# First batch of an FFT filter with a routed expert layer: logits from the spectrum, one index chain, gates in four chunks

## The chip, the cores and the metric

One core of a Trainium2 chip runs the whole program. Its engines are TensorE (PE, with its weight loads as PEld), VectorE (DVE), ScalarE (ACT), GpSimd (POOL) and SyncE (SP, which here only starts transfers). The metric is the device time of one execution in microseconds, as the median of three runs. One further execution was profiled, and its trace gives the rows below.

## What is computed

```
X = rfft(x, axis=1)                      # x: 8 batches x 2496 tokens x 256
y = irfft(X * (filt_r + 1j*filt_i))      # 19968 rows of 256
xn, en = y / |y|, emb / |emb|            # 8 experts
logits = xn @ en.T / tau
e = argmax(logits); gate = softmax(logits)[e]
out = gate * (relu(y @ w1[e]) @ w2[e])   # w1: 256x1024, w2: 1024x256 per expert
```

## The kernel before

**Stages of a batch.** The program handles the eight batches as groups 0 to 7. The transform is a mixed-radix product: `conv_s1` multiplies the input by a table (tiles `s`), `conv_s2` transforms again (`s`, `xs`, `yy`), multiplies by the filter and transforms back (`sa`), and `conv_sb` makes the rows. A group has 11 tiles of two blocks (22 blocks of up to 117 tokens). For each tile `conv_sb` takes a block of the filtered spectrum (`vt`, 120 frequencies by 512), makes `y` by the product with the table `csb` (fp32), sums the squares on ACT into `ssq` (L795), takes a power-of-two scale `rr` from them with two small DVE operations (`q`, `rr`, L798 and L800), and writes the row as a high half (ACT, L766) and a low half in fp16 (DVE, L769). Eight PE transposes turn the tile (`tp`, L828), DVE copies it out (`yT`, L830), and eight small fp16 products with the normalised experts (`ent`, `enz`) give the logits `lp` (L843).

**Routing.** `route` works on a chunk of tiles. The index chain on DVE finds the maximum, a one-hot `oh`, the rank of each row in its expert (products `rk` on PE, L931 to L934), and the row number `ixi`. The gates need the norm of the row: `norm_steps` (L165 to L181) is a chain of small dependent operations, followed by f, d, an exp on ACT, `se` and a reciprocal (L952). Then POOL scatters the rows to `XS` in DRAM, two indirect transfers per tile, 22 per group (L965). In group 0 the constant `FIRST` cuts the 11 tiles into chunks of 3, 4 and 4; the norms of the first two chunks run on POOL (`gates(nc.gpsimd)`), that of the last on DVE.

**Experts.** Each group then has eight expert slots of 256 rows: SP reads the rows back transposed (`xT`, L1101), PE makes `ph` with the first weights (L1134), ACT and DVE make the two halves of `h` (L1140, L1141), PE makes `po` (L1162), and the result goes out by POOL. Each slot has four parts, so that ph_2_1 is the second part of slot 2.

**Weights.** The weights of each expert come as fp32 and are cut into fp16 halves once. `weight_halves` does it in small steps: maxima (`wmx` on DVE L288, `wj` on ACT L285), a product `pm` that transposes them (L295), a product `ps` that spreads them (L305), then the high halves (ACT, L325) and low halves (DVE L330; for one of the four pieces POOL, L323 and L328).

**What sets the order.** In group 0 nothing leaves the chip between the first product and the rows: `conv_first` keeps the spectrum in `turned`, and `turn_back` (L620) transposes it block by block (`v`, copied to `vt` by ACT, L623). `head()` runs 35 steps of `conv_first`, then `conv_sb(0)`, and from a given step on (`S1AT`) also the first stage of group 1, `conv_s1(1)`. For the head the program's order is the engines' order for ACT, PE, DVE and SP. `WLOADS` and `PREPS` list the steps after which a weight load or a preparation step is issued. After the head a planner with costs of its own places the slots, the stages of the next group and what is left of the preparation, one preparation step at each call of `spread`.

Of the kernel before, what the change touches and what calls it, by code (L numbers as in the profile page):

```python
# [43 lines left out]
FIRST = (0, 3, 7, 11)  # L44
# [11 lines left out]
PREPS = (21, 25, 46, 48, 51, 53, 58, 58, 59, 60, 63, 63, 63, 63, 64, 64, 66, 67, 67, 68, 68, 69, 70, 70)  # L56
S1AT = 62
# [3 lines left out]
def moe_spectral_kernel(  # L61
# [125 lines left out]

    def experts_ready():
# [26 lines left out]
        nc.vector.tensor_copy(enz[:, :, 0:E], ept[:, 0:2, 0:E])  # L215
        yield
# [215 lines left out]
    def load(q, g, pool, tag, t, ap, rows, full):  # L432
        if pool is rowp:
            it = pool.tile([P, 2, ROW], F16, tag="rows", name=f"{tag}{g}_{t}").rearrange("p j c -> p (j c)")
            it = it.bitcast(F32)[:, :2 * D].rearrange("p (j c) -> p j c", j=2)
        else:
            it = pool.tile([P, 2, D], F32, tag=tag, name=f"{tag}{g}_{t}")
        got = []
        for h, k, m in whole(g, ap, t, rows, full):
            q.dma_start(it[:k, h], m)  # L440
            got.append((h, it[:k, h].rearrange("p j c -> p (j c)")))
        return got
# [273 lines left out]

    def conv_sb(g):
# [4 lines left out]
        def load_v(t):  # L722
            return load(nc.sync, g, cf, "f", t, buf_at(g, ZD[g]), freqs, 120) if g else turn_back(t)

        ahead = 3 if g else 1
        if g:
            yield W_GAP
        vin = {t: load_v(t) for t in range(ahead)}
        if g:
            yield W_GAP  # L730
        parts, out_rows = [], []
        starts = FIRST if g == 0 else tuple(range(0, NTL, CHUNK)) + (NTL,)
# [8 lines left out]
        def part():  # L741

            if parts and next(parts[0], None) is None:
                parts.pop(0)
            for _ in range(len(out_rows) if g == 0 else min(1, len(out_rows))):
                out_rows.pop(0)()
# [3 lines left out]
        for s in range(NTL + LPL):  # L750
# [22 lines left out]
            if t < NTL:  # L773
                c, at, n = chunk(t)
                if at == 0:
# [12 lines left out]
                y = (ps_o if g == 0 and t % 3 == 2 else ps_y).tile(  # L788
                    [P, 2, D], F32, tag="o" if g == 0 and t % 3 == 2 else "y", name=f"y{g}_{t}")
# [12 lines left out]
                if g == 0 and u + 2 == n:  # L802
                    sg, n0, f = (rt.tile([P, NTC], F32, tag=tag, name=f"{tag}0_{t}")[:, :n] for tag in ("sg", "n0", "f"))

                    def gates(w, sg=sg, n0=n0, f=f, ssq=ssq[:, :n], rr=rr[:, :n]):
                        for _ in norm_steps(sg, ssq, n0, w):
                            pass
                        w.tensor_tensor(out=sg, in0=sg, in1=rr, op=ALU.mult)
                        w.tensor_scalar(out=f, in0=sg, scalar1=tau64, scalar2=None, op0=ALU.mult)
# [10 lines left out]
            if g == 0 and s == NTL + 1:  # L820
                gates(nc.vector)
# [32 lines left out]
    def route(g, out_rows, t0, n, rows, ssq, rr, lp, f=None):  # L854
# [12 lines left out]
        def bc(t):  # L867
            return t.unsqueeze(2).to_broadcast([P, nt, E])
# [5 lines left out]
        if g:  # L874
            sg, n0, f = sm("sg"), sm("n0"), sm("f")
        norm = norm_steps(sg, ssq, n0) if g else iter(())
# [14 lines left out]
        if g:  # L891
            yield 1
# [13 lines left out]
        if g:  # L906
            v.scalar_tensor_tensor(out=f, in0=sg, scalar=tau64, in1=rr, op0=ALU.mult, op1=ALU.mult)
            v.reciprocal(f, f)
            v.tensor_tensor(out=d, in0=d, in1=bc(f), op=ALU.mult)
        ex = big("ex")  # L910

        def gates():
            if g == 0:
                v.reciprocal(f, f)
                v.tensor_tensor(out=d, in0=d, in1=bc(f), op=ALU.mult)
            nc.scalar.activation(ex, d, AF.Exp)

        late = g == 0 and not part_
        if late:
            yield 1  # L920
        else:
            gates()
            if g:
                yield 1
# [18 lines left out]
        if g == 0:  # L943
            v.tensor_copy(ixi, ix)
        if late:
            gates()
            yield 1
# [6 lines left out]
        def rows_out(u, k):  # L954

            if g:
                with behind("conv"):
                    v.tensor_copy(ixi[:, u:u + 1], ix[:, u:u + 1])
            scatter_rows(g, rows[u // 2][:k, u % 2].bitcast(I32), ixi[:k, u:u + 1])
# [239 lines left out]
    def head():  # L1199
        yield from conv_first()  # L1200
        s1 = conv_s1(1)
        next(s1)
        n = 0
        for w in conv_sb(0):
            yield w
            n += 1
            if n > S1AT - 35:
                next(s1, 0)
        yield from s1
# [173 lines left out]
```

## Time and profile before

| | |
|---|---|
| median of three runs (1399.37 to 1404.8) | 1400.31 us |
| the profiled execution | 1404.15 us |
| its span in the trace | 1402.2 us |
| PE busy | 1282.1 us, 91% |
| DVE, ACT, POOL busy | 901.4, 745.9, 548.1 us |

The span runs from the first to the last instruction; the profiled execution's own time is 2 us more. Busy time of PE counts a matmul from its start to a modelled end, so a stretch with 100% need not be at PE's peak. The granted clock is given as a share of the upper level of 2.4 GHz; 0.50 is the lower level, 1.2 GHz.

### The profile page before, as it was taken

How to read it: one execution, taken by the hardware profiler on the slowest of the kernel's cores; microseconds unless marked ns; L12 is line 12 of the kernel's file. 1: busy time of each engine (PE TensorE's matmuls, PEld its weight loads, DVE VectorE, ACT ScalarE, POOL GpSimd, SP SyncE). 2: the span in 40 equal slices, each digit the busy share in tenths (PEclk: the TensorE clock that was granted, in tenths of full speed). 3: DMA queues.
4: the chain of work that ended last, by engine and by line, in shares of the span. 5: the costliest groups of instructions: out<-in, count | busy, mean ns of one | idle time of the engine just before them, and what ended most of it. 6: DMA issues, size and time to landing. Idle time of an engine off the chain costs nothing. (4 is left out here: it accounts for less than half of the span.)

```text
span 1402.2 us, 32774 instructions
## 1 busy us (share of the span) xinstructions
PE 1282.1 (91%) x11308; PEld 1017.4 (73%) x11308; DVE 901.4 (64%) x2850; ACT 745.9 (53%) x1714; POOL 548.1 (39%) x622
## 2 busy tenths in 40 slices
PE   8858999579989997999899989998999899999997
PEld 6535666346767886788687768776787678999997
DVE  3777669554757695758576858685768532366664
ACT  5755377255626773767376737673665223333332
POOL 3363334634353334443543454345423532222221
PEclk9967999889999998999899989998999999999999
DMA  9838855567657664876487557754762322221221
GB/s 326 296 115 245 247 144 154 171 181 212 182 159 188 194 174 138 217 181 193 135 238 182 173 147 209 200 169 133 215 161 64 88 76 46 50 52 48 47 51 35
DMA packets 223256, 218.77 MB, mean 156 GB/s; under 512 B 125022, under 2 KB 168445, under 8 KB 221164
## 3 DMA queue, kind: packets, MB, share of 16 engines
q1 hardware_dynamic: 194491, 156.06, 41.3%
q0 software_dynamic: 25584, 57.79, 13.5%
q10 hardware_dynamic: 3009, 2.75, 0.6%
q8 instruction: 94, 1.54, 0.5%
q14 instruction: 78, 0.64, 0.2%
HBM read 116.43 MB, written 79.60 MB: 140 GB/s over the span
## 5 line engine op out<-in xcount | busy, mean ns | idle before, releaser
L1162 PE MATMUL po<-W,h 128*128 128x256 f16 (+1 forms) x3864 | 522.9, 279 | 22.6 <-issue 21.9
L1162 PEld LDWEIGHTS <-h 128*128 128x128 f16 x3864 | 371.5, 100 | 121.2 <-issue 75.1
L1134 PE MATMUL ph<-xT,W 128*128 128x256 f16 x3072 | 410.5, 279 | 30.0 <-issue 14.9
L1140 ACT ACTIVATE h<-ph 128x512 f16<-128x512 f32 (+1 forms) x388 | 204.1, 528 | 328.7 <-PE ph L1134 156.1
L1134 PEld LDWEIGHTS <-W 128*128 128x128 f16 x3072 | 297.1, 100 | 111.9 <-issue 73.7
L1141 DVE SCALAR_TENSOR_TENSOR h<-ph,h 128x512 f16<-128x512 f32 (+1 forms) x388 | 231.7, 598 | 210.9 <-ACT h L1140 174.5
L1066 POOL DMA_INDIRECT out_dram<-o,meta x161 | 172.7, 1073 | 350.4 <-ACT o L1169 297.7
L965 POOL DMA_INDIRECT XS<-rows,ixi x176 | 179.1, 1018 | 147.3 <-issue 90.9
L693 POOL TENSOR_TENSOR yy<-yy,xs 128x512 f32<-128x512 f32 x48 | 68.4, 1425 | 124.6 <-DVE xs L658 83.1
L440 POOL DMA_DIRECT2D in<-in_x x72 | 56.3, 783 | 131.3 <-PE s L480 47.3
L1134 PE MATMUL ph<-xT,wp 128*128 128x128 f16 x1584 | 104.9, 219 | 0.0
L1134 PEld LDWEIGHTS <-wp 128*128 128x128 f16 x1584 | 96.7, 98 | 2.7 <-issue 0.2
L1169 ACT ACTIVATE o<-po,meta 128x256 f32<-128x256 f32 x161 | 69.9, 477 | 32.9 <-PE po L1162 22.7
L1120 DVE COPY wp<-W 128x1024 f16 x132 | 58.2, 441 | 44.1 <-PE ph L1134 43.2
L766 ACT ACTIVATE rows<-y,rr 128x256 f16<-128x256 f32 x176 | 74.2, 485 | 20.1 <-DVE rr L800 15.9
L769 DVE SCALAR_TENSOR_TENSOR rows<-y,rr,rows 128x256 f16<-128x256 f32 x176 | 76.7, 478 | 12.4 <-ACT rows L766 11.0
L656 DVE TENSOR_TENSOR yy<-s,f 128x256 f32<-128x256 f32 x140 | 53.1, 419 | 39.4 <-ACT xs L686 20.4
L795 ACT ACTIVATE rows<-y 128x256 f16<-128x256 f32 x176 | 66.7, 393 | 19.0 <-PE y L480 11.5
L516 ACT COPY s<-s 128x512 f32<-128x512 f32 x74 | 43.9, 598 | 61.1 <-PE s L480 19.8
L830 DVE COPY yT<-tp 128x1024 f16<-128x1024 f16 x88 | 60.3, 685 | 16.4 <-remote 12.6
L828 PE MATMUL tp<-ident,rows 128*128 128x128 f16 x704 | 63.8, 224 | 4.2 <-issue 1.6
L828 PEld LDWEIGHTS <-rows 128*128 128x128 f16 x704 | 48.2, 100 | 21.6 <-issue 15.7
(244 smaller groups left out, 1763.9 us busy)
## 6 DMA issues: line engine op xcount, KB each, us to landing
f<-in_filt SPq DMA_DIRECT2D x148, 256.0 KB
a<-SD SPq DMA_DIRECT2D x70, 256.0 KB
ZD<-z SPq DMA_DIRECT2D x70, 256.0 KB
f<-ZD SPq DMA_DIRECT2D x70, 240.0 KB
W<-in_w SPq DMA_DIRECT2D x15, 1024.0 KB
SD<-s SPq DMA_DIRECT2D x60, 240.0 KB
in<-in_x POOLq DMA_DIRECT2D x60, 234.0 KB
in<-in_x SPq DMA_DIRECT2D x20, 234.0 KB
```

The lines of the kernel that those rows point to most:

```text
L693: (nc.vector if k < 2 else nc.gpsimd).tensor_tensor(out=yy, in0=yy, in1=xs, op=ALU.add)
L766: nc.scalar.activation(rows[:, i, 0:D], y[:, i], AF.Copy, scale=rr[:, u:u + 1])
L769: last["conv"] = nc.vector.scalar_tensor_tensor(out=rows[:, i, D:2 * D], in0=y[:, i], scalar=rr[:, u:u + 1], in1=rows[:, i, 0:D], op0=ALU. ...
L795: nc.scalar.activation(rows[:, i, D:2 * D], y[:, i], AF.Square, accum_out=ssq[:, u + i:u + i + 1])
L828: nc.tensor.transpose(tp[:, i, j], rows[:, i, j * P:(j + 1) * P], ident)
L965: i = nc.gpsimd.indirect_dma_start(out=XS, out_offset=bass.IndirectOffsetOnAxis(ap=ix, axis=0), in_=src, in_offset=None)
L1066: i = nc.gpsimd.indirect_dma_start(out=out, out_offset=bass.IndirectOffsetOnAxis(ap=idx, axis=0), in_=o, in_offset=None, bounds_check=NT - ...
L1134: last["pe"] = nc.tensor.matmul(ph[:, fi, :size], wp[:, k * 2 + wh, fi * P:(fi + 1) * P], xT[:, xh * 2 + k], start=(c == 0), stop=(c == 5))
L1140: last["relu"] = nc.scalar.activation(h[:, 0, :, :size], ph[:, :, :size], AF.Relu)
L1141: hd = nc.vector.scalar_tensor_tensor(out=h[:, 1, :, :size], in0=ph[:, :, :size], scalar=0.0, in1=h[:, 0, :, :size], op0=ALU.max, op1=ALU. ...
L1162: nc.tensor.matmul(self.po[:, s], self.hs[fp][:, hh, fi, s * P:(s + 1) * P], self.Wp[:, off + wh * 1024:off + wh * 1024 + D], start=(fp == ...
L1169: nc.scalar.activation(o, self.po[:, s], AF.Copy, scale=self.meta[:, s, 1:2])
```

## The change

The logits of group 0 no longer come from the rows. The normalised experts are kept in fp32 and transposed (`e32`); for each block of the spectrum two fp32 products give `Lp` (120 frequencies by 8 experts), 44 in all; DVE copies `Lp` out and one product with `csb` gives the unscaled logits of all 22 blocks at once (`lp`, 128 by 176). One index chain covers all blocks. It starts beside tile 0 and its steps alternate with those of the first chunk's norm. The transposes `tp`, the copies `yT` and the products with `ent` and `enz` go for group 0. The gates are made in four chunks of 2, 3, 3 and 3 tiles, with all norms on DVE. `PREPS` has 16 entries instead of 24: in the head come the maxima of expert 1 and all of expert 0, and the halves of expert 1 and the maxima of expert 2 move behind the head. `S1AT` goes from 62 to 57.

```diff
-FIRST = (0, 3, 7, 11)
+FIRST = (0, 2, 5, 8, 11)
-PREPS = (21, 25, 46, 48, 51, 53, 58, 58, 59, 60, 63, 63, 63, 63, 64, 64, 66, 67, 67, 68, 68, 69, 70, 70)
-S1AT = 62
+PREPS = (21, 25, 44, 48, 51, 53, 55, 57, 58, 59, 59, 60, 61, 62, 64, 66)
+S1AT = 57
...
+        ep32 = ps_r.tile([P, 2, E], F32, tag="r", name="ep32")
+        for k in range(2):
+            nc.tensor.transpose(ep32[:, k], esc[:, k * P:(k + 1) * P], ident32[0:E, 0:E])
+        nc.vector.tensor_copy(e32, ep32)
...
+    def conv_sb_first():
...
+        Lp = ps_c.tile([P, n, E], F32, tag="c", name="Lp")
+        def spectrum(us):
+            for u in us:
+                k = freqs(u)
+                for half in range(2):
+                    nc.tensor.matmul(Lp[:k, u], turned[1][:, half, u * 120:u * 120 + k], e32[:, half],
+                                     start=(u == 0 and half == 0), stop=(u == n - 2 and half == 1))
+        def logits():
+            v.tensor_copy(lt_[0:120, 0:n - 1], Lp[0:120, 0:n - 1])
+            v.tensor_copy(lt_[0:40, n - 1], Lp[0:40, n - 1])
+            lp = ps_r.tile([P, n, E], F32, tag="r", name="lp0")
+            nc.tensor.matmul(lp.rearrange("p t e -> p (t e)"), csb_sb, lt_[0:120].rearrange("p t e -> p (t e)"),
+                             start=True, stop=True)
+            return lp
+        def index():
...
+            nc.tensor.matmul(rkf[:, 0], lt16, ohf, start=True, stop=False)
+            nc.tensor.matmul(rkf[:, 1], one16, ohf, start=False, stop=False)
+            for j in range(1, n):
+                nc.tensor.matmul(rkf[:, 0, j * E:], one16, ohf[:, 0:(n - j) * E], start=False, stop=(j == n - 1))
...
+        def norm(u):
+            yield from norm_steps(sg[:, u], ssq[:, u], n0[:, u])
+            yield v.tensor_scalar(out=f[:, u], in0=sg[:, u], scalar1=tau64, scalar2=None, op0=ALU.mult)
+            yield v.reciprocal(f[:, u], f[:, u])
...
+        chain = index()
+        vin = {0: turn_back(0)}
+        spectrum(range(0, 12))
+        due = []
+        for s in range(NTL + 1):
+            if s + 1 < NTL:
+                vin[s + 1] = turn_back(s + 1)
+            if s == 0:
+                spectrum((*range(12, n - 2), n - 1, n - 2))
...
+            yield W_SB
+            ready = due.pop(0) if due else None
+            if ready:
+                u, out_tiles = ready
+                v.tensor_tensor(out=d[:, u], in0=d[:, u], in1=bc(f[:, u]), op=ALU.mult)
...
+                if ready:
+                    nc.scalar.activation(ex[:, u], d[:, u], AF.Exp)
...
+            if ready:
+                v.tensor_reduce(out=se[:, u], in_=ex[:, u], axis=AX.X, op=ALU.add)
+                v.scalar_tensor_tensor(out=se[:, u], in0=se[:, u], scalar=1e-9, in1=rr[:, u], op0=ALU.add,
+                                       op1=ALU.mult)
+                for j in out_tiles:
+                    v.reciprocal(rows[j].bitcast(F32)[:, :, D + 1:D + 2], se[:, 2 * j:2 * j + 2].unsqueeze(2))
+                    rows_out(j)
...
+            if t + 1 in FIRST:
+                a = FIRST[FIRST.index(t + 1) - 1]
+                u = slice(2 * a, 2 * t + 2)
+                steps = norm(u)
+                due.append((u, range(a, t + 1)))
+            for _ in range(3 if s == 0 else 99):
+                if [next(i, chain) for i in (chain, steps)] == [chain, chain]:
+                    break
+            yield W_SB
...
-                    if t + 1 < NTL:
-                        gates(nc.gpsimd)
-                    ck["f"] = f
...
-        for w in conv_sb(0):
+        for w in conv_sb_first():
```

The order of instructions shows the move at three places. PE's order where `conv_sb` of group 0 begins (`W` is here the tile that holds `turned`), before:

```order
L620 MATMUL v_0_616<-ident_140,W 120x128 x4
L620 MATMUL v_1_623<-ident_140,W 120x128 x4
L480 MATMUL y_0_633<-vt_0_617,csb_sb 128x512
L620 MATMUL v_2_642<-ident_140,W 120x128 x4
L480 MATMUL y_1_654<-vt_1_624,csb_sb 128x512
L620 MATMUL v_3_663<-ident_140,W 120x128 x4
L480 MATMUL y_2_675<-vt_2_643,csb_sb 128x512
```

and after, where `aside_0` holds `e32` and the copied `Lp`:

```order
L636 MATMUL v_0_625<-ident_140,W 120x128 x4
L760 MATMUL Lp<-aside_0_170,W 120x8 x24
L636 MATMUL v_1_656<-ident_140,W 120x128 x4
L760 MATMUL Lp<-aside_0_170,W 120x8 x16
L760 MATMUL Lp<-aside_0_170,W 40x8 x2
L760 MATMUL Lp<-aside_0_170,W 120x8 x2
L496 MATMUL y_0_684<-vt_0_626,csb_sb 128x512
L767 MATMUL lp_694<-aside_0_170,csb_sb 128x176
L636 MATMUL v_2_699<-ident_140,W 120x128 x4
L496 MATMUL y_1_707<-vt_1_657,csb_sb 128x512
```

The 44 products stand as 88 instructions, since `order` counts each fp32 product as two; all of them are ahead of the first y, and the product lp stands between y_0 and y_1.

DVE's order around tiles 5 and 6, where a chunk's norm begins (L165 to L168), before:

```order
L769 SCALAR_TENSOR_TENSOR rows_5_809<-y_5_810,rr_3_728,rows_5_809 128x256 x2
L798 TENSOR_SCALAR q_6_870<-ssq_3_727 128x2
L800 TENSOR_SCALAR rr_3_728<-q_6_870 128x2
L165 TENSOR_SCALAR ssq_3_727<-ssq_3_727 128x8
L166 TENSOR_SCALAR n_6_874<-ssq_3_727 128x8
L168 TENSOR_SCALAR sg_6_873<-n_6_874 128x8
L936 TENSOR_TENSOR l_0_905<-rk_0_897,ecap 128x48
L937 TENSOR_TENSOR l_0_905<-l_0_905,oh_0_858 128x48
L939 TENSOR_REDUCE ix_0_909<-l_0_905 128x6
L941 TENSOR_REDUCE tot_0_906<-rk_0_897 128x8
L942 TENSOR_TENSOR base_0_896<-ecap,tot_0_906 128x8
L944 CAST ixi_0_911<-ix_0_909 128x6
```

and around tile 4 after the change, where the slots of `aside_2` hold ssq, sg, f and se:

```order
L854 SCALAR_TENSOR_TENSOR rows_3_810<-y_3_811,aside_2_172,rows_3_810 128x256 x2
L868 TENSOR_SCALAR q_4_840<-aside_2_172 128x2
L869 TENSOR_SCALAR aside_2_172<-q_4_840 128x2
L165 TENSOR_SCALAR aside_2_172<-aside_2_172 128x6
L166 TENSOR_SCALAR aside_2_172<-aside_2_172 128x6
L168 TENSOR_SCALAR aside_2_172<-aside_2_172 128x6
...
L180 TENSOR_TENSOR aside_2_172<-aside_2_172 128x6
L181 TENSOR_SCALAR aside_2_172<-aside_2_172 128x6
L812 TENSOR_SCALAR aside_2_172<-aside_2_172,tau_169 128x6
L813 RECIPROCAL aside_2_172<-aside_2_172 128x6
L845 TENSOR_TENSOR aside_0_170<-aside_0_170,aside_2_172 128x48
L854 SCALAR_TENSOR_TENSOR rows_4_830<-y_4_831,aside_2_172,rows_4_830 128x256 x2
```

Before, DVE gives three operations of a norm and POOL the rest; after, the whole norm stands on DVE between two tiles' low halves.

ACT's order between the last part of slot 1 and slot 2 (L325 and L341 make high halves, L285 and L301 maxima), before:

```order
L1140 ACTIVATE h_1_3_1872<-ph_1_3_1859 128x512
L325 ACTIVATE W<-W,wsc 128x1024 x2
L713 COPY z_1_1584<-sa_1_1581 128x512
L1140 ACTIVATE h_2_0_1910<-ph_2_0_1897 128x512
L325 ACTIVATE W<-W,wsc 128x1024
L325 ACTIVATE W<-W 128x1024
L713 COPY z_2_1622<-sa_2_1619 128x512
L1140 ACTIVATE h_2_1_1973<-ph_2_1_1956 128x512
```

and after:

```order
L1266 ACTIVATE h_1_3_1645<-ph_1_3_1632 128x512
L301 ACTIVATE wj_0_1385,wmx<-W 128x1024
L729 COPY z_2_1369<-sa_2_1366 128x512
L301 ACTIVATE wj_1_1387,wmx<-W 128x1024
L1295 ACTIVATE o_1_0_1778<-po_1_1610,meta_1_1168 128x256
L1295 ACTIVATE o_1_1_1780<-po_1_1610,meta_1_1168 128x256
L729 COPY z_3_1406<-sa_3_1403 128x512
L729 COPY z_4_1446<-sa_4_1443 128x512
L341 ACTIVATE W<-W,wsc 128x1024 x3
L301 ACTIVATE wj_0_1493,wmx<-W 128x1024
L729 COPY z_5_1479<-sa_5_1476 128x512
L301 ACTIVATE wj_1_1495,wmx<-W 128x1024
```

After the change the maxima of experts 2 and 3 and the halves of expert 2 stand between the relu of slot 1 and that of slot 2, which comes two rows below the last row shown.

## Rows read from the trace of the kernel before

**Rows 1.** The first two lines of the page: span, and busy time of each engine.

```profile
span 1402.2 us, 32774 instructions
PE 1282.1 (91%) x11308; PEld 1017.4 (73%) x11308; DVE 901.4 (64%) x2850; ACT 745.9 (53%) x1714; POOL 548.1 (39%) x622
```

**Rows 2.** Busy time by stretch, core 0; the line ahead of the rows names the columns.

```profile
core 0: us, PE busy (x) PEld busy (x) DVE busy (x) ACT busy (x) POOL busy (x), PEclk, DMA share, GB/s
50.00:75.00 25.00, 20.58 (x172) 12.76 (x169) 17.12 (x69) 20.25 (x68) 9.45 (x35) 0.93 0.56 227
75.00:100.00 25.00, 15.48 (x106) 8.45 (x106) 17.95 (x78) 12.52 (x28) 13.06 (x19) 0.59 0.29 84
110.00:120.00 10.00, 7.68 (x12) 2.24 (x10) 9.69 (x9) 6.63 (x10) 6.19 (x4) 0.65 0.81 211
130.00:140.00 10.00, 10.00 (x73) 7.19 (x72) 9.90 (x20) 7.06 (x11) 0.94 (x1) 1.00 0.93 301
250.00:300.00 50.00, 27.88 (x172) 16.84 (x172) 23.89 (x99) 15.50 (x28) 20.77 (x22) 0.76 0.45 130
```

**Rows 3.** Timeline of DVE: start, length in us, line, operation, tiles, count, idle time before.

```profile
52.50 0.17 DVE L798 TENSOR_SCALAR q<-ssq 128x2 int32<-128x2 int32 x1 [5.42 <-ACT rows L795]
53.79 0.88 DVE L769 SCALAR_TENSOR_TENSOR rows<-y,rr,rows 128x256 f16<-128x256 f32 x2 [0.91 <-ACT rows L766]
55.85 0.88 DVE L769 SCALAR_TENSOR_TENSOR rows<-y,rr,rows 128x256 f16<-128x256 f32 x2 [0.91 <-ACT rows L766]
57.39 0.69 DVE L830 COPY yT<-tp 128x1024 f16<-128x1024 f16 x1
86.84 0.16 DVE L165 TENSOR_SCALAR ssq<-ssq 128x8 f32<-128x8 f32 x1
89.91 0.23 DVE L809 TENSOR_SCALAR f<-sg,tau 128x8 f32<-128x8 f32 x1
97.97 0.35 DVE L952 RECIPROCAL rows<-se 128x2 f32<-128x2 f32 x4
```

**Rows 4.** Timeline of the weight loads (PEld), same columns.

```profile
49.14 0.85 PEld L620 LDWEIGHTS v<-ident,W 128*120 128x120 f32 x8 [0.97 <-ACT W L609]
58.13 0.27 PEld L843 LDWEIGHTS <-yT 128*128 128x128 f16 x8 [1.24 <-DVE yT L830]
```

**Rows 5.** Timeline of PE, same columns.

```profile
50.47 1.13 PE L480 MATMUL y<-vt,csb_sb 120*128 120x512 f32 x2 [0.24 <-ACT vt L623]
65.93 0.22 PE L931 MATMUL rk<-oh,lt 128*128 128x48 f16 x1 [1.98 <-DVE oh L904]
66.02 0.30 PE L934 MATMUL rk<-oh,one 128*128 128x40 f16 x5
```

**Rows 6.** Timeline of POOL: the last two scatters of the group.

```profile
108.23 0.99 POOL L965 DMA_INDIRECT XS<-rows,ixi  x1 [0.30 <-issue]
109.52 0.90 POOL L965 DMA_INDIRECT XS<-rows,ixi  x1 [0.30 <-issue]
```

**Rows 7.** Timeline of PE and SP up to the first expert.

```profile
105.76 0.58 PE L295 MATMUL pm<-ident,wmx 128*4 128x128 f32 x2 [4.92 <-issue]
113.32 3.78 PE L480 MATMUL s<-in,c_sb 117*128 117x512 f32 x4 [0.74 <-DVE s L514]
120.65 0.58 PE L295 MATMUL pm<-ident,wmx 128*4 128x128 f32 x2 [1.02 <-DVE wmx L288]
121.92 0.58 PE L305 MATMUL ps<-wdg,one 4*128 4x2 f32 x2 [0.69 <-DVE wdg L298]
122.43 1.89 PE L1134 MATMUL ph<-xT,W 128*128 128x256 f16 x8
114.95 1.35 SPq L1101 DMA_TRANSPOSE xT<-XS  x1
```

**Rows 8.** Timeline of ACT: the four high halves of one expert.

```profile
85.21 4.25 ACT L325 ACTIVATE W<-W,wsc 128x1024 f16<-128x1024 f32 x4
```

**Rows 9.** Timeline of PE where the second batch takes over.

```profile
288.04 2.72 PE L1134 MATMUL ph<-xT,W 128*128 128x256 f16 x12 [9.78 <-DVE h L1141]
```

More of the change, by code (lines that the diff above doesn't have):

```diff
@@ L186, in moe_spectral_kernel, with place @@
     tau64 = const.tile([P, 1], F32, tag="tau64", name="tau64")
+    aside0 = [cy.tile([P, 2, 4, P], F16, tag="yT", name=f"aside0_{i}").rearrange("p i j c -> p (i j c)").bitcast(F32)
+              for i in range(3)]
+    places = {}
+    def place(nm, i, w):
+        at = places.get(i, 0)
+        places[i] = at + w
+        return aside0[i][:, at:at + w]
+    e32 = place("e32", 0, 2 * E).rearrange("p (k e) -> p k e", k=2)
     def experts_ready():
@@ L722, in load_v @@
         def load_v(t):
[L723 to L727, printed above, removed]
+            return load(nc.sync, g, cf, "f", t, buf_at(g, ZD[g]), freqs, 120)
+        ahead = 3
+        yield W_GAP
         vin = {t: load_v(t) for t in range(ahead)}
-        if g:
-            yield W_GAP
+        yield W_GAP
         parts, out_rows = [], []
-        starts = FIRST if g == 0 else tuple(range(0, NTL, CHUNK)) + (NTL,)
+        starts = tuple(range(0, NTL, CHUNK)) + (NTL,)
         chunks = {}
@@ L744, in part @@
                 parts.pop(0)
-            for _ in range(len(out_rows) if g == 0 else min(1, len(out_rows))):
+            if out_rows:
                 out_rows.pop(0)()
@@ L787, in conv_sb @@
                 u = at * 2
-                y = (ps_o if g == 0 and t % 3 == 2 else ps_y).tile(
-                    [P, 2, D], F32, tag="o" if g == 0 and t % 3 == 2 else "y", name=f"y{g}_{t}")
+                y = ps_y.tile([P, 2, D], F32, tag="y", name=f"y{g}_{t}")
                 for h, vt in vin.pop(t):
@@ L801, in conv_sb @@
                                         scalar2=194.0 * 2.0 ** 23, op0=ALU.mult, op1=ALU.add)
[L802 to L809, printed above, removed]
-                    if t + 1 < NTL:
-                        gates(nc.gpsimd)
-                    ck["f"] = f
                 (b, ag), _ = tiles(g, t)
@@ L819, in conv_sb @@
             part()
-            if g == 0 and s == NTL + 1:
-                gates(nc.vector)
             t = s - 2
@@ L852, in conv_sb, with route @@
             yield from zero_rows(state["base"])
-    def route(g, out_rows, t0, n, rows, ssq, rr, lp, f=None):
+    def route(g, out_rows, t0, n, rows, ssq, rr, lp):
         tg = f"{g}_{t0}"
@@ L873, in route @@
         mx, se, mv = sm("mx"), sm("se"), sm("mv")
-        if g:
-            sg, n0, f = sm("sg"), sm("n0"), sm("f")
-        norm = norm_steps(sg, ssq, n0) if g else iter(())
+        sg, n0, f = sm("sg"), sm("n0"), sm("f")
+        norm = norm_steps(sg, ssq, n0)
         def norms(k):
@@ L890, in route @@
         v.scalar_tensor_tensor(out=ws, in0=d, scalar=0.0, in1=w8b, op0=ALU.is_ge, op1=ALU.mult)
-        if g:
-            yield 1
+        yield 1
         norms(2)
@@ L905, in route @@
         norms(8)
[L906 to L909, printed above, removed]
+        v.scalar_tensor_tensor(out=f, in0=sg, scalar=tau64, in1=rr, op0=ALU.mult, op1=ALU.mult)
+        v.reciprocal(f, f)
+        v.tensor_tensor(out=d, in0=d, in1=bc(f), op=ALU.mult)
         ex = big("ex")
[L912 to L924, printed above, removed]
+        nc.scalar.activation(ex, d, AF.Exp)
+        yield 1
         base = state["base"]
@@ L942, in route @@
         v.tensor_tensor(out=nbase, in0=base, in1=tot, op=ALU.add)
[L943 to L947, printed above, removed]
         v.tensor_reduce(out=se, in_=ex, axis=AX.X, op=ALU.add)
@@ L954, in rows_out @@
         def rows_out(u, k):
-            if g:
-                with behind("conv"):
-                    v.tensor_copy(ixi[:, u:u + 1], ix[:, u:u + 1])
+            with behind("conv"):
+                v.tensor_copy(ixi[:, u:u + 1], ix[:, u:u + 1])
             scatter_rows(g, rows[u // 2][:k, u % 2].bitcast(I32), ixi[:k, u:u + 1])
```

81 lines of the change are left out of this document (added).

## The prediction

> **What bounds the kernel now.** I read the page first: PE is busy for 1282 of 1402 us, no other engine for more than 65% [rows 1]. The windows then show where PE is not full. From 130 us on it is full at the upper clock level (10.00 of 10 us, granted 1.00), but while group 0's rows are made it is not: 20.58 of 25 us from 50, 15.48 of 25 from 75 and 7.68 of 10 from 110, the last two at a granted clock of 0.59 and 0.65, that is, mostly at 1.2 GHz [rows 2]. So nearly all of PE's work after the first expert product (122.43 us [rows 7]) is one block that starts when the head is done. The change is worth what it moves the first expert product, plus any gap that it opens or closes behind it. The other such place is the hand-over to group 1: PE busy 27.88 of 50 us from 250 [rows 2], with one idle time of 9.78 us before a `ph` [rows 9].
>
> Next I read the timelines of the stretch of rows. A tile takes 2.06 us (low halves at 53.79 and 55.85 [rows 3]), and DVE waits 0.91 us in it for ACT's high half. PE's transposes and logit products, which the change removes, are not what a tile waits for. The last gates are done at 97.97 + 0.35 = 98.3 [rows 3], the last scatter at 109.52 + 0.90 = 110.4 [rows 6], the transposed load of the first slot starts at 114.95, and the first `ph` is released by the chain `pm` 120.65, `ps` 121.92, `ph` 122.43, on weights, not on rows [rows 7].
>
> **The change, part by part.**
>
> *The 44 fp32 products `Lp`.* They are 88 instructions with a weight load each, all ahead of `y_0` on PE. Eight loads of the same form (120 columns, fp32) take 0.85 us, 0.106 each; eight fp16 loads take 0.27 us, 0.034 each [rows 4]. By the first the products take 88 x 0.106 = 9.4 us, by the second 3.0. I take 9.4, the row of the same shape and type, at nearly the same time. At the lower level of the clock it would be twice that, 18.7. Today PE has nothing to do there but wait for copies, yet `y_0` stands behind the products in PE's order, and all of DVE's row work behind `y_0`; so the whole 9.4 us is on the path, and `y_0` starts at 50.47 + 9.4 = 59.9 [rows 5].
>
> For matmuls with few columns the Trainium skill ("TensorE: Matmul & The Clock Gate", section "Wait — 56ns, not 53.3ns?") gives a start-to-start time that never falls below about 25 ns. By that floor alone, an estimate, the 88 would take 2.2 us and the total below would be 7 us lower. The load row shows 106 ns instead, so here the load, not the floor, should set the pace.
>
> *DVE's work from `y_0` to the last gates.* Removed are 11 copies `yT` of 0.69 us [rows 3], 7.6 us, and three index chains. Added are one index chain, two copies of `Lp`, and the norms that POOL did. A norm is 16 dependent operations at 0.205 us (first at 86.84, last at 89.91 [rows 3]), 3.3 us; four norms take 13 us where DVE did one and a fraction. First chunk: `q` comes 2.0 us after `y` starts (50.47 to 52.50 [rows 3, 5]), at 61.9. Then come two copies and the product `lp` (2 us), some 18 index operations of 0.2 to 0.35 us (5 us), 23 rank products with 2200 columns in all (two products of 48 columns start 0.09 us apart [rows 5], so 2.1 us, and 0.4 for the hand-over), the ten norm operations not hidden between index operations (2 us), two low halves (1.8), the wait for `y_1`, which PE makes behind `lp` (1.5), and d, se and reciprocals (1.0): 15.8, so the first gates are at 77.7. A later chunk of three tiles: two tiles at 2.06, the third's low half and its q and rr (1.28), the norm (3.3), d, se and reciprocals (1.0): 9.7. Three of them: 29.1. The last gates come at 106.8 against 98.3: 8.5 us later, almost all of it the price of `Lp`. What DVE saves in copies it pays back in norms.
>
> *Scatters.* They run at 1.30 us each (108.23, 109.52 [rows 6]). The last chunk now has six: 106.8 + 7.8 = 114.6, 4.2 us later than before. The load of the first slot follows 4.5 us after the last scatter now (110.4 to 114.95), so it starts at 119.1. Before, the first `ph` came 7.5 us after that load, but released by the weights; so the load takes between 1.35 and 7.5 us, and by this path `ph` is at 120.5 to 126.6.
>
> *Group 1's first stage.* In ACT's order the copy of the second `s` stands behind the last chunk's exp, so nine of its eleven products follow 106.8. Two take 3.78 us today (113.32 [rows 7]), 1.9 each at the lower level: 17 us, to 123.9. At the upper level it is half, 8.6, to 115.4, and then DVE's halves and the row path decide. `pm` to `ph` adds 1.8 us (120.65 to 122.43 [rows 7]). So the stage ends at 117 to 126. Here PE works without a gap, as it did not before (7.68 of 10 us), so the clock may rise in it. From both paths I take `ph` at 124.5: **2 us later**. `S1AT` by itself costs nothing: the first `s` is hidden behind the last chunk.
>
> *Preparation moved behind the head.* Eight steps leave the head, where ACT has room (12.52 of 25 us from 75 [rows 2]). Expert 1's halves fit beside slot 0. Expert 2's chain starts only after the relu of slot 1's last part: two maxima on ACT (about 1.06 us each, as a high half of the same size: 4.25 for four [rows 8]), `pm`, `ps` and scale (1.9, from 120.65 to about 122.5 [rows 7]), four high halves (4.25), and in between expert 3's two maxima (2.1): 10.4 us before the weights of slot 2 are whole. PE has meanwhile the end of slot 1's `po` (12 products at 0.14, 73 records in 10 us [rows 2], 1.6) and six or seven convolution products of 1.13 [rows 5], about 7: a gap of about 2 us, and about as much again before `ph_2_2`, where expert 3's `pm` stands. I take **4 us**; the bounds are 0 (the planner's other work covers it) and 8 (both at their worst).
>
> *Taken out of PE:* 88 transposes and 88 small logit products. They lay in the stretch where PE waits, so I count nothing for them. If PE set the pace there they would give some 10 us back; the 0.91 us by which DVE waits for ACT in each tile [rows 3] says that it does not.
>
> **Sum.** 2 + 4 = +6 us. Against the profiled execution, 1404.15, that is 1410; that execution lies 3.8 above the median 1400.31, so the median after comes to **1406 us**. Half a per cent, 7 us, is about what a measurement of this kernel can tell from no change; so "faster" is below 1393.3 and "slower" above 1407.3.
>
> **Rivals.**
>
> - *Cheap products.* Loads pass in the shadow of the matmuls, at the pace of the fp16 row: 3.0 us instead of 9.4. The last gates are then at 100, the scatters end at 108, earlier than today, and `ph` comes at about 117 to 120. With a gap of 0 to 4 us in slot 2 the time is 1396 to 1402. For it: a `v` of eight fp32 products overlaps loads and matmuls already. Against it: their loads take 0.106 each all the same. Chance 0.15.
> - *The hand-over to group 1 gets better.* The planner places all of group 1 anew after the head. If group 1's last rows come earlier relative to slot 7, the 9.78 us [rows 9] and smaller gaps beside it, some 14 us, shrink. At full recovery: 1406 - 14 = 1392, and it decides the sign from 13 us on. Against it: in PE's order the last `y` of group 1 stands at the same place beside the products of slot 6, and its last rank product just ahead of slot 7's, before and after. Chance 0.13.
> - *`Lp` at the lower level of the clock.* PE idles while it waits for `sa` and copies, and 75 to 100 already shows 0.59 [rows 2]. Another 9.3 us: 1413 to 1416. Against it: 50 to 75 shows 0.93. Chance 0.13.
> - *Preparation stays late.* Each further expert repeats the gap, since its chain also starts one slot later. Two more gaps of 2 to 4: 1410 to 1414. Against it: from slot 3 on the preparation steps in the order stand where they stood. Chance 0.10.
> - *As summed.* `ph` between 121 and 127 and a gap of 0 to 8 give 1400 to 1412 for it alone. Chance 0.49.
>
> **Numbers.** Faster by over 0.5%: nearly all of the second rival at its full size and the lowest corner of the first, 0.18. Slower: the third and fourth, and the part of the likeliest above 1407.3 (a good third), 0.40. The rest, 0.42, is no change that can be told. The range leaves out the extremes of the second rival and the upper end of the third: 1392 to 1417.
>
> **What would show it.** Right: about 9 us from the first `Lp` to `y_0` on PE, last gates at 105 to 109, last scatter near 115, first `ph` at 121 to 127, a gap before `ph_2_0`. Wrong: `Lp` done in 3 us or in 19; the first `ph` before 120; PE full through slots 1 to 3; the gap before 288 us gone or moved; gaps in slots behind 3.

## The result

| | before | after |
|---|---|---|
| median of 11 runs | 1402.3 us | 1411.09 us |
| range of the runs | 1394.89 to 1406.93 | 1404.42 to 1416.18 |
| profiled execution | 1404.15 us | 1416.18 us |

The ratio after to before is 1.0068, with an interval of 1.0044 to 1.0093: slower by 0.7%, or 9.5 us. The profiled execution of after is the slowest of its 11, so its rows are read for where time lies, and the size of the loss is taken from the ratio.

The first two lines of the page of after, to be held against [rows 1]:

```profile
span 1414.4 us, 32601 instructions
PE 1297.8 (92%) x11222; PEld 1025.9 (73%) x11222; DVE 898.5 (64%) x2858; ACT 745.0 (53%) x1715; POOL 539.6 (38%) x590
```

The windows of after, with the columns of [rows 2]:

```profile
49.00:50.00 1.00, 0.60 (x3) 0.60 (x4) 0.00 (x0) 0.35 (x1) 0.00 (x0) 0.77 0.93 369
50.00:75.00 25.00, 23.36 (x105) 20.56 (x104) 1.32 (x6) 2.60 (x7) 0.00 (x0) 0.50 0.40 164
130.00:140.00 10.00, 7.43 (x21) 3.65 (x21) 3.54 (x13) 3.25 (x6) 1.50 (x1) 0.50 0.86 201
250.00:300.00 50.00, 39.05 (x357) 29.03 (x356) 37.51 (x166) 24.28 (x58) 31.98 (x32) 0.92 0.57 165
```

From 50 to 75 us PE is now busy nearly throughout, and the granted clock is 0.50 where it was 0.93. DVE, which had 17.12 us of work there [rows 2], has 1.32. From 130 to 140, where PE was full, it is still in the head. The hand-over (250 to 300) has become better: 39.05 us of PE work for 27.88.

PE at the start of the rows in after (start, length, line, operation, tiles, count):

```profile
49.40 1.03 PE L636 MATMUL v<-ident,W 128*120 128x128 f32 x4 [0.78 <-ACT W L625]
50.23 9.62 PE L760 MATMUL Lp<-aside,W 128*120 128x8 f32 x48
60.58 7.69 PE L760 MATMUL Lp<-aside,W 128*120 128x8 f32 x40
68.12 2.06 PE L496 MATMUL y<-vt,csb_sb 120*128 120x512 f32 x2
```

The 88 instructions take 9.62 + 7.69 us, 0.197 each, and `y_0` starts at 68.12 where it started at 50.47 [rows 5]. The clock had fallen before the first of them: from 49 to 50 us it is already 0.77 on average, in a stretch where PE waits for copies between short bursts (0.78 us ahead of `v`, of which four take 1.03 us here and 0.65 in e2). The products run at the lower level from the first to the last. On DVE, the first and last operation of the third chunk's norm and the last reciprocals of the group:

```profile
101.73 0.16 DVE L165 TENSOR_SCALAR aside<-aside 128x6 f32<-128x6 f32 x1
105.07 0.19 DVE L813 RECIPROCAL aside<-aside 128x6 f32<-128x6 f32 x1
117.05 0.29 DVE L862 RECIPROCAL rows<-aside 128x2 f32<-128x2 f32 x3
```

From the first to the last operation of the norm it is 3.3 us, against 3.1 in [rows 3]; the last gates are done at 117.05 + 0.29 = 117.3 where [rows 3] has 98.3. The way to the first `ph` in after, on PE, ACT, POOL and SP:

```profile
108.25 3.78 PE L496 MATMUL s<-in,c_sb 117*128 117x512 f32 x4
...
117.76 5.48 PE L496 MATMUL s<-in,c_sb 117*128 117x512 f32 x8 [3.16 <-ACT s L532]
...
136.32 0.59 PE L311 MATMUL pm<-ident,wmx 128*4 128x128 f32 x2 [0.75 <-ACT wj L301]
137.54 0.58 PE L321 MATMUL ps<-wdg,one 4*128 4x2 f32 x2 [0.62 <-DVE wdg L314]
138.05 4.55 PE L1260 MATMUL ph<-xT,W 128*128 128x256 f16 x24
130.86 0.58 ACT L532 COPY s<-s 128x512 f32<-128x512 f32 x1 [6.09 <-DMA SD<-s]
125.93 0.89 POOL L1091 DMA_INDIRECT XS<-rows,aside  x1 [0.30 <-issue]
131.30 1.71 SPq L1227 DMA_TRANSPOSE xT<-XS  x1
```

The last scatter ends at 126.8 (110.4 in [rows 6]), the load of the first slot starts 4.5 us later, and the first `ph` at 138.05 for 122.43 [rows 7]: **15.6 us later**. Group 1's first stage takes from 108.25 to 135.6, with waits for copies of `s`, which wait in turn for the stores of `s` to DRAM (6.09 us in one case).

How far the loss carries is read from the output transfers on POOL. The first output of slot 2 and the first of slot 7, which is the last slot of group 0 and comes out behind the hand-over, in the kernel before:

```profile
183.21 1.05 POOL L1066 DMA_INDIRECT out_dram<-o,meta  x1 [2.88 <-ACT o L1169]
311.12 1.02 POOL L1066 DMA_INDIRECT out_dram<-o,meta  x1 [0.21 <-issue]
```

and in after:

```profile
217.67 1.08 POOL L1192 DMA_INDIRECT out_dram<-o,meta  x1 [0.31 <-issue]
324.20 1.01 POOL L1192 DMA_INDIRECT out_dram<-o,meta  x1 [0.20 <-issue]
```

At slot 2 after is 34.5 us late, at slot 7 13.1 us (as is group 1's first output, 341.58 for 328.50), at the end of the span 12.2 (1414.4 to 1402.2). The windows from the first `ph` to slot 2's output, before and after:

```profile
122.40:183.20 60.80, 60.80 (x380) 41.56 (x381) 39.03 (x78) 27.51 (x44) 18.29 (x12) 0.96 0.81 242
138.05:217.67 79.62, 72.53 (x412) 46.67 (x412) 55.58 (x100) 40.93 (x63) 26.53 (x17) 0.93 0.63 197
```

In the kernel before PE is busy throughout; in after it is idle for 7.1 us. So slot 2 has the gap that was forecast. But PE also does 33.7 us of group 1's transform in this time for 26.6 (`s` and `sa`), and with that and the better hand-over more than the gap comes back.

### The profile page after: what moved, and what is told of

The parts are those of the page before. It is cut to its first block, busy times and chain, and to the rows that moved or that the text cites. A ratio compares the mean times of both kernels' runs of the same rounds, so it can differ in the third digit from the quotient of the medians.

```text
span 1414.4 us, 32601 instructions
## 1 busy us (share of the span) xinstructions
PE 1297.8 (92%) x11222; PEld 1025.9 (73%) x11222; DVE 898.5 (64%) x2858; ACT 745.0 (53%) x1715; POOL 539.6 (38%) x590
## 5 line engine op out<-in xcount | busy, mean ns | idle before, releaser
L1288 PE MATMUL po<-W,h 128*128 128x256 f16 (+1 forms) x3864 | 517.4, 276 | 30.2 <-issue 28.4
L1288 PEld LDWEIGHTS <-h 128*128 128x128 f16 x3864 | 367.1, 99 | 125.9 <-issue 82.6
L1091 POOL DMA_INDIRECT XS<-rows,ixi x154 | 156.1, 1014 | 130.3 <-issue 83.4
L929 ACT ACTIVATE rows<-y,rr 128x256 f16<-128x256 f32 x154 | 65.1, 484 | 22.8 <-DVE rr L962 18.3
L932 DVE SCALAR_TENSOR_TENSOR rows<-y,rr,rows 128x256 f16<-128x256 f32 x154 | 67.2, 477 | 9.3 <-ACT rows L929 7.6
L957 ACT ACTIVATE rows<-y 128x256 f16<-128x256 f32 x154 | 58.3, 393 | 18.1 <-PE y L496 12.2
L977 DVE COPY yT<-tp 128x1024 f16<-128x1024 f16 x77 | 52.7, 684 | 14.1 <-remote 7.2
L469 ACT CAST yp<-yy 128x512 fp32r<-128x512 f32 x50 | 30.9, 618 | 56.9 <-POOL yy L709 51.5
L470 DVE TENSOR_TENSOR yp<-yy,yp 128x512 fp32r<-128x512 f32 x50 | 36.5, 730 | 33.6 <-ACT yp L469 29.2
```

The costliest lines, as they stand in the source:

```text
L929: nc.scalar.activation(rows[:, i, 0:D], y[:, i], AF.Copy, scale=rr[:, u:u + 1])
L932: last["conv"] = nc.vector.scalar_tensor_tensor(out=rows[:, i, D:2 * D], in0=y[:, i], scalar=rr[:, u:u + 1], in1=rows[:, i, 0:D], op0=ALU. ...
L957: nc.scalar.activation(rows[:, i, D:2 * D], y[:, i], AF.Square, accum_out=ssq[:, u + i:u + i + 1])
L1091: i = nc.gpsimd.indirect_dma_start(out=XS, out_offset=bass.IndirectOffsetOnAxis(ap=ix, axis=0), in_=src, in_offset=None)
L1288: nc.tensor.matmul(self.po[:, s], self.hs[fp][:, hh, fi, s * P:(s + 1) * P], self.Wp[:, off + wh * 1024:off + wh * 1024 + D], start=(fp == ...
```

## The experiments

Each ratio is to the kernel before, measured beside it, over five rounds, with its 95% interval. The kernel before had a median of 1398.6 us beside e1 to e4, of 1410.7 beside e5 to e8 and of 1308.0 to 1308.7 beside e9 to e12, so ratios of one group are compared among themselves first. The changed kernel itself was measured in none of these groups, but beside a kernel before of 1402.3 us.

**e1: the products alone, in the kernel before.**

```diff
+                if g == 0 and t == 0:
+                    spectrum_only()
                 for h, vt in vin.pop(t):
...
```

`spectrum_only` makes the 44 products into a tile that nobody reads.

> The kernel before with one part of the change alone: e32 and the 44 products Lp ahead of y_0 on PE; nothing reads Lp, the logits come from the rows as before. Theory A (the products hold the whole head, at the lower clock level): Lp takes 17 to 19 us, y_0 moves from 50.5 to 68 us, the first ph from 122.4 to 135 to 140, and the time grows by 11 to 16 us (ratio to the kernel before 1.008 to 1.011). Theory B (the later preparation and the norms on DVE cost more than the products): first ph before 130, ratio under 1.004.

Measured: 1413.49 us, ratio 1.011 (1.0073 to 1.0146). PE in e1, the products, `y_0` and the first `ph`:

```profile
51.57 13.93 PE L729 MATMUL Lp<-e,W 128*120 128x8 f32 x88
65.35 2.05 PE L486 MATMUL y<-vt,csb_sb 120*128 120x512 f32 x2
137.19 4.44 PE L1151 MATMUL ph<-xT,W 128*128 128x256 f16 x24
```

In this execution the products took 13.9 us, not the 17 to 19 of theory A: they began at the upper level (granted clock 1.00 from 50 to 54 us) and went on at the lower one (0.58 from 54 to 62). `y_0` is 14.9 us late and the first `ph` 14.8. So theory A holds for the head: what the products take goes through it undiminished. That it goes on into the time rests on the median, 14.8 us above the kernel before's. The execution with the trace is the fastest of its six, and its span of 1403.7 us ends only 1.5 us behind [rows 1], so no row shows the rest of the way.

**e5: the same number of products, eight times as wide.**

```diff
-    e32 = place("e32", 0, 2 * E).rearrange("p (k e) -> p k e", k=2)
+    e32 = place("e32", 2, 16 * E).rearrange("p (k e) -> p k e", k=2)
...
```

The experts stand in it eight times over, 64 columns; `Lp` is now three tiles, copied out in four operations instead of two.

> The changed kernel with e32 repeated eight times along its columns: each of the 44 products has 64 columns instead of 8, seven eighths of the result are not read. Weight loads, order and all else stay. Theory C (the clock falls because PE's columns are few while the products run): the granted clock stays at 0.9 or more from 50 to 62 us, the products take 9 to 11 us instead of 17.7, y_0 starts at 59 to 62, the first ph at 128 to 132, ratio to the kernel before 1.000 to 1.004. Theory D (the loads' pace or the waits before set it, not the columns): products 17 to 20 us, first ph 136 to 140, ratio 1.005 to 1.010.

Measured: ratio 1.0013 (0.998 to 1.0047). PE in e5, and its window from 50 to 62 us:

```profile
51.11 5.15 PE L761 MATMUL Lp<-aside,W 128*120 128x64 f32 x48
56.54 4.38 PE L761 MATMUL Lp<-aside,W 128*120 128x64 f32 x40
60.76 1.08 PE L496 MATMUL y<-vt,csb_sb 120*128 120x512 f32 x2
```

```profile
50.00:62.00 12.00, 11.22 (x98) 10.24 (x98) 0.00 (x0) 1.86 (x4) 0.00 (x0) 1.00 0.87 358
```

Eight times the columns in 9.5 us instead of 17.3, at a granted clock of 1.00 instead of 0.50, and `y_0` at 60.76. The first `ph` is at 128.3. Against after the wide ones bring `y_0` 7.4 us and the first `ph` 9.8 us back; the ratio is 0.55 points lower, between two groups whose intervals just touch.

That the columns matter is read best against e1, where PE has the same waits ahead of the products as in e5: there the clock fell under the narrow ones, here it stayed up through all of the wide ones. In e2 (below) the products are those of after, and they too began at the upper level:

```profile
50.72 6.29 PE L760 MATMUL Lp<-aside,W 128*120 128x8 f32 x48
57.74 7.69 PE L760 MATMUL Lp<-aside,W 128*120 128x8 f32 x40
```

The 48 take 0.131 us each, the 40 then 0.192, at a granted clock of 1.00 from 50 to 54 us and 0.59 from 54 to 56. So theory C holds for e1, e2 and e3, where the clock falls while PE is busy with narrow products. In after and e7 it fell before the first of them, and only stayed down. With 64 columns it stayed up in e5, e9 and e10; in e6 it had fallen ahead of `y_0` and was up again as the first piece began (0.57 from 50 to 54 us, 1.00 from 54 to 56). Begun at the upper level the narrow products take 13.9 us (e1) and 14.0 (e2), begun at the lower one 17.3 (after), and the wide ones take 9.5 (e5). By these rows, an estimate, some 3 of the 7.4 us between after and e5 are the chance of an execution.

**e3: the narrow products in three pieces behind y_0, y_1 and y_2.**

```diff
-        spectrum(range(0, 12))
+        share = (range(0, 8), range(8, 16), (*range(16, n - 2), n - 1, n - 2))
...
-FIRST = (0, 2, 5, 8, 11)
+FIRST = (0, 3, 6, 9, 11)
...
                 yp[t] = y
+                if s < len(share):
+                    spectrum(share[s])
```

> The changed kernel with the 44 products in three pieces behind y_0, y_1 and y_2, the index chain behind the third, and gate chunks of 3, 3, 3 and 2 tiles. Theory A: y_0 is back at 50.5 us, DVE has work from 52 us on, the products run between the wide y products at a granted clock above 0.75, the last gates come at 101 to 105 instead of 117, the first ph at 112 to 120 instead of 138, and the time falls to 0.992 to 0.999 of the kernel before. Theory B (norms on DVE and preparation set the head): last gates after 110, first ph after 128, ratio over 1.003.

Measured: 1409.91 us, ratio 1.0075 (1.0048 to 1.0103). `y_0` was back at 51.6 us, as theory A said, but the last gates came at 112.9 and the first `ph` at 133.9. These numbers and the ratio are theory B's; its cause (norms and preparation) is not what the rows show. The three pieces on PE:

```profile
52.54 4.38 PE L760 MATMUL Lp<-aside,W 128*120 128x8 f32 x32
59.36 6.42 PE L760 MATMUL Lp<-aside,W 128*120 128x8 f32 x32
68.22 4.49 PE L760 MATMUL Lp<-aside,W 128*120 128x8 f32 x24
```

The first begins at the upper level (32 in 4.38 us), the others run at the lower one (32 in 6.42, 24 in 4.49). The single `y` products between the pieces did not bring the clock back, the last piece ends at 72.7 us, later than in after, and no gate can be made before it.

**e2 and e4: the preparation steps.** e2 is the changed kernel with eight entries added to `PREPS`, e4 the kernel before with only 16:

```diff
-PREPS = (21, 25, 44, 48, 51, 53, 55, 57, 58, 59, 59, 60, 61, 62, 64, 66)
+PREPS = (21, 25, 44, 48, 51, 53, 55, 57, 58, 59, 59, 60, 61, 62, 62, 63, 63, 64, 64, 65, 65, 66, 66, 66)
```

```diff
-PREPS = (21, 25, 46, 48, 51, 53, 58, 58, 59, 60, 63, 63, 63, 63, 64, 64, 66, 67, 67, 68, 68, 69, 70, 70)
+PREPS = (21, 25, 46, 48, 51, 53, 58, 58, 59, 60, 63, 63, 64, 66, 68, 70)
```

> The changed kernel with the eight preparation steps (halves of expert 1, maxima of expert 2) back in the head. Theory A (products): the gap in slot 2 shrinks, the first ph stays at 137 to 142, the time stays within 3 us of the changed kernel (ratio to the kernel before 1.004 to 1.010). Theory B (late preparation): 5 to 9 us come back, ratio 0.999 to 1.003.

> The kernel before with 16 entries in PREPS, so that the halves of expert 1 and the maxima of expert 2 come behind the head as in the change; all else as before. Theory A: first ph up to 4 us earlier, a gap in slot 2 of about the same size, ratio 0.997 to 1.003. Theory B: the gap is not won back, ratio 1.004 to 1.008.

Measured: e2 1425.24 us, ratio 1.0174 (1.0138 to 1.0209); e4 1393.61 us, ratio 0.9947 (0.9917 to 0.9976). Both theories missed the sign: putting the steps back costs about one point (e2 against after, which stands in another group). In e2 the last `pm` of the head waits 4.36 us for maxima on DVE:

```profile
137.72 0.58 PE L311 MATMUL pm<-ident,wmx 128*4 128x128 f32 x2 [4.36 <-DVE wmx L304]
```

In e4, the first `ph` and the first outputs of slot 2 and of slot 7:

```profile
117.08 4.32 PE L1134 MATMUL ph<-xT,W 128*128 128x256 f16 x24
188.36 1.08 POOL L1066 DMA_INDIRECT out_dram<-o,meta  x1 [9.56 <-ACT o L1169]
303.23 1.02 POOL L1066 DMA_INDIRECT out_dram<-o,meta  x1 [0.21 <-ACT o L1169]
```

The head is 5.3 us shorter (122.43 in [rows 7]), slot 2 is 5.2 us later than before's 183.21, and slot 7 is 7.9 us earlier than its 311.12. The 5.3 us are about the 4.92 us that the first `pm` in [rows 7] waits for nothing that the profile shows. With 24 entries e1 and e2 have the same wait (5.19 and 3.82 us); with 16 the head has one `pm` fewer and no such wait.

**e7 and e8: group 1's first stage earlier**, in the changed kernel (`S1AT` 49 for 57) and in e4 (56 for 62).

> The changed kernel with S1AT 49 instead of 57: group 1's first stage begins four tiles earlier, between the tiles of the rows. Theory E (that stage lasts 27 us because its loads and stores wait for transfers, and it sets the first ph): s_0 at 92 to 97 instead of 108, first ph 4 to 5 us earlier (133 to 134, then the scatters set it), ratio 1.002 to 1.005. Theory F (the rows set the head, and the earlier products get in their way): last gates 2 to 5 us later, first ph unchanged or later, ratio 1.006 to 1.012.

> The kernel before with 16 entries in PREPS and S1AT 56 instead of 62. Theory E: group 1's first stage ends 3 to 6 us earlier, but the scatters end at 110 as before, so the first ph comes at 114 to 117 (116.8 us with PREPS alone), ratio 0.992 to 0.996. Theory F: the last gates come 2 to 5 us later, first ph at 118 to 122, ratio 0.996 to 1.000.

Measured: e7 1.0092 (1.0056 to 1.0127), e8 1.0087 (1.0052 to 1.0121). In e7 the stage is done at 121.6 us, and then `ph` waits for its rows; the two PE rows:

```profile
117.55 4.08 PE L496 MATMUL s<-in,c_sb 117*128 117x512 f32 x6 [2.54 <-ACT s L532]
134.14 4.27 PE L1260 MATMUL ph<-xT,W 128*128 128x256 f16 x24 [12.51 <-DMA xT<-XS]
```

In e7 the last gates come at 120.8, 3.5 us later than in after. In e8 DVE's copy of `s` waits for a store and holds the last chunk's gates behind it (98.3 in [rows 3]), and `ph` waits for the rows again:

```profile
100.85 0.69 DVE L514 COPY s<-s 128x512 f32<-128x512 f32 x1 [6.08 <-DMA SD<-s]
105.60 0.35 DVE L952 RECIPROCAL rows<-se 128x2 f32<-128x2 f32 x4
121.93 4.09 PE L1134 MATMUL ph<-xT,W 128*128 128x256 f16 x24 [11.37 <-DMA xT<-XS]
```

So the stage and the scatters end close together; starting the one earlier delays the other, as theory F said. In e7 the first `ph` was still 3.9 us earlier, as theory E said, and the kernel was not faster. e8 is slower than either theory allowed.

**e6, e9, e10: wide products in three pieces**, with `S1AT` 53, with 57, and with 57 and the first chunk's norm on POOL:

```diff
-        def norm(u):
+        def norm(u, w):
-            yield from norm_steps(sg[:, u], ssq[:, u], n0[:, u])
+            yield from norm_steps(sg[:, u], ssq[:, u], n0[:, u], w)
...
-                steps = norm(u)
+                steps = norm(u, nc.gpsimd if t + 1 <= FIRST[1] else v)
```

> The 64-column products in three pieces behind y_0, y_1 and y_2 with gate chunks of 3, 3, 3 and 2 tiles, and group 1's first stage four steps earlier (S1AT 53). Theory C: clock above 0.85 from 50 to 75 us, first scatter at 74 to 78 us instead of 88, last gates at 100 to 104, first ph at 118 to 126, ratio 0.992 to 0.998. Theory D: clock at 0.5 to 0.65, first scatter after 82, ratio 1.003 to 1.008.

> As e6_spread_wide, with S1AT back at 57. Theory E2 (the earlier first stage of group 1 holds DVE and ACT with its waits for stores while rows are made, and turns the later hand-over worse): last gates 2 to 4 us earlier than in e6, first ph at 117 to 121, ratio 0.993 to 0.998. Theory F2 (the position of that stage is not the cause): ratio 1.003 to 1.007 as in e6.

> As e9, with the norm of the first chunk of three tiles on POOL, which has nothing to do before the first scatter. Theory G (DVE's row work is what the head waits for once the products are cheap): DVE is free 3 us earlier, first ph 2 to 3 us earlier than in e9, ratio 0.001 to 0.003 below e9. Theory H (the first stage of group 1 and the scatters set it): no change against e9.

Measured: e6 1.0047 (1.0023 to 1.0072), e9 1.0088 (1.0063 to 1.0112), e10 1.0098 (1.0074 to 1.0122). In e9 the last reciprocals on DVE, and on PE the end of the first stage and `ph`:

```profile
103.64 0.23 DVE L865 RECIPROCAL rows<-aside 128x2 f32<-128x2 f32 x2
117.35 4.08 PE L496 MATMUL s<-in,c_sb 117*128 117x512 f32 x6 [1.40 <-ACT s L532]
123.91 5.30 PE L1263 MATMUL ph<-xT,W 128*128 128x256 f16 x24
```

The last gates are done at 103.9, 13.5 us earlier than in after, yet the first `ph` is at 123.9, 1.5 us behind [rows 7] and 3 us behind theory E2, since group 1's first stage ends at 121.4. The head was brought back to nearly its old length, not below it. These 1.5 us are little beside the 0.88% (some 11 us) that e9 loses in its group. Where the rest lies is not shown, since this group has no trace of the kernel before. In e10 the gates of the first chunk come no earlier and the last at 103.8, with the first `ph` at 122.8: that norm on DVE is not what is waited for (theory H). e6, whose first stage starts earlier, has its last gates at 108.4, 4.5 us behind e9, as theory E2 said of the gates (about 1 us of it lies ahead of them, since `y_0` ran at the lower level in e6). Its first `ph` is at 121.5, where theory C had put it, but its ratio is the one of theory D; that e9's ratio would be lower than e6's did not come true, in another group.

**e11 and e12: four chunks on top of e4, and e4 once more.** e11 has `FIRST = (0, 3, 6, 9, 11)` in e4's kernel.

> The kernel before with 16 entries in PREPS (e4) and its gates in chunks of 3, 3, 3 and 2 tiles: the four chunks of the change without the spectrum's logits. The last chunk leaves four scatters instead of eight behind the last gates. Theory G: one more index chain costs DVE and PE 3 to 5 us, last gates later, scatters end within 2 us of 110, ratio 0.994 to 1.000. Theory H (scatters of the last chunk set it): scatters end 3 to 5 us earlier, first ph at 113 to 116, ratio 0.990 to 0.995.

> The kernel of e4 once more (the kernel before with 16 entries in PREPS), because e11, which differs from it only in its gate chunks, came out slower than the kernel before, though its first ph is only 2 us later than in e4. Theory I (the four chunks cost it): e4's gain comes again, ratio 0.992 to 0.998. Theory J (the gain of the shorter preparation in the head depends on the execution: on how long the hand-over to group 1 takes in the kernel before): ratio 0.998 to 1.008 with the first ph again at 115 to 119.

Measured: e11 1.0064 (1.0044 to 1.0084), e12 1.0037 (1.0016 to 1.0058). In e12 the first `ph`, the first outputs of slot 2 and of slot 7, and the window from 300 to 600 us:

```profile
119.34 4.46 PE L1134 MATMUL ph<-xT,W 128*128 128x256 f16 x24
190.86 1.08 POOL L1066 DMA_INDIRECT out_dram<-o,meta  x1 [9.57 <-ACT o L1169]
302.12 1.02 POOL L1066 DMA_INDIRECT out_dram<-o,meta  x1 [0.22 <-ACT o L1169]
300.00:600.00 300.00, 295.99 (x2503) 234.47 (x2501) 213.28 (x678) 193.69 (x451) 141.30 (x160) 1.00 0.74 201
```

and that window in e4, the same kernel:

```profile
300.00:600.00 300.00, 283.88 (x2305) 218.79 (x2303) 197.94 (x645) 175.11 (x407) 133.81 (x148) 0.97 0.70 188
```

The head and the first group go as in e4 (`ph` at 119.3, slot 7 at 302.1), but from 300 to 600 PE is busy for 295.99 us at a clock of 1.00, where e4 had 283.88 at 0.97. One difference can be read: the view of waits lists 74 idle times of PE in e4, 45.8 us in all, which it puts down to "issue", that is, to nothing that the profile shows, and not one in e9 to e12. The largest group of them in e4 (total us, times, longest us):

```profile
PE po L1162 <- issue: 24.7, 44, 1.1
```

The trace of the kernel before has 82 of them, 59 us. What makes them is not shown. Beside executions like e12's the kernel before takes 1308 us, and the shorter preparation is no gain. So theory J's range holds: the gain of e4 is there beside e1 to e3, and absent in e12. A trace of the kernel before beside e12 would be needed to see where its hand-over differs; there is none, so this stays open. e11 is slower than e12 by 0.27 points with overlapping intervals: four chunks give nothing. Its scatters end at 109.1 us, as theory G said, and its ratio is above both theories.

## Why the prediction was right, and where its terms were not

The forecast was 1406 us in 1392 to 1417, +6 us, with 0.40 on slower and 0.42 on no change that can be told; measured were 1411.09 us and +9.5. Direction, size and range held, but two terms were wrong in opposite directions, and that they cancelled in part is luck. By most of the signs that the prediction set itself it was wrong: the products took 17.3 us for about 9, the last gates came at 117.3 for 105 to 109, the last scatter ended at 126.8 for near 115, and the first `ph` came at 138.05 for 121 to 127.

- **"I take 9.4, the row of the same shape and type."** This step failed. The load row [rows 4] was right for the upper level: e5 took 9.5 us. The products took 17.3 at the lower level, near the price that the third rival gave (18.7), at a chance of 0.13. Its reason, that PE idles for `sa` and copies, fits after, where the clock fell in just that stretch; e1 and e2 show that narrow products that begin at the upper level lose it too. The argument against that rival, 0.93 from 50 to 75 us, came from a stretch with products of 512 columns; the products that replace them have 8. That row could not speak for them.
- **The floor of 25 ns per matmul** (the Trainium skill, "TensorE: Matmul & The Clock Gate", section "Wait — 56ns, not 53.3ns?") did not come into play: e5's 40 products at the upper level took 4.38 us, 110 ns each.
- **From y_0 to the last gates** 46.9 us were forecast and 49.2 measured, the last scatters took 9.5 us for the 7.8 forecast, and the 4.5 us to the load came as said. Norms on DVE cost what rows showed (3.3 us for 3.1 between first and last start), and e10 shows that moving one away gives nothing.
- **Group 1's first stage** ends 18.2 us after the last gates, where 9 to 17 follow from the prediction, and the first `ph` comes after 20.7, where 10 to 19 do. The forecast priced PE's rate; what the stage waits for are copies held by stores. That `S1AT` "costs nothing" was too simple: e7 and e8 show that an earlier start costs.
- **"I take 4 us" for the late preparation.** This step failed in sign. The gap is there (7.1 us of idle PE up to slot 2's output, within the bounds of 0 to 8), but I counted nothing for the work taken out of the head, and took the gap as lost. In e4 the head is 5.3 us shorter, and part of slot 2's delay is group 1's transform done earlier, which came back at the hand-over. In the changed kernel it is worth 1.06 points (e2 to after, between groups), some 15 us. As e4 and e12 show, nearly a point of such an effect can come and go between groups.
- **The sum.** The first `ph` was put 2 us late and was 15.6 late; behind it +4 was forecast, and 3.4 came back (15.6 to 12.2). The second rival, a better hand-over, came true in part: 39.05 us of PE work from 250 to 300 for 27.88. Nor is PE's work behind the head one full block, as the prediction took it: in the trace of the kernel before PE is busy for 281.56 us from 300 to 600, at a granted clock of 0.97.

In ratio points, as differences of measured ratios that add up by their making: the products +1.1 (e1), about half of it the clock (after against e5, 0.55), the rest of the new routing about +0.6 (e2 against e1, with intervals that overlap), the shorter preparation about -1.1. Only e1 and e2 stand in one group.

No version here is faster than the kernel before everywhere: e4 is, by 0.5%, beside e1 to e3, and is 0.4% slower in its second measurement.

## What to carry to other kernels

Before work moves to an engine that seems to have room, look at what stands behind it in that engine's order: PE waited in this stretch, but everything waited for PE's first product. A duration from the trace holds for the clock of its own stretch; where many narrow matmuls replace wide ones, price them at the lower level too, or make them wider, which made them faster here. A level of the clock seen in one execution need not be that of the next: ahead of the same products it had fallen in after and e7 and not in e1, e2 and e3. And steps deferred out of a start-up phase are worth what they take there, if the gap that they leave later can be filled with other work.

## What was not expected of the hardware

Under 88 matmul instructions of 8 columns, with PE busy without a gap, the granted clock fell to 0.50 (e1, e2, e3) or stayed there (after, e7, 0.197 us each). It did not fall under the same 88 with 64 columns (e5, about 0.11 us each). The Trainium skill ("TensorE: Matmul & The Clock Gate", section "HAM oscillation — how this bites in real kernels") ties the fall of the clock in a kernel to gaps in which PE idles. In after it fell where PE waits between bursts (0.78 us ahead of `v`). In e1 and e2 it fell with PE busy, after waits like those that e5 has ahead of its products too, so the measurement adds that being busy with few columns did not keep the clock up here. The same kernel in two sets of runs took 1393.61 and 1312.55 us (e4, e12), with mean granted clocks of 0.957 and 0.978 in their profiled executions.
